# Linear attention and a gated MLP: q loaded in runs of eight tokens on 64 partitions per head, with the remaining token of each run in a chunk of its own

## The chip, the cores and the metric

One core of a Trainium2 chip runs the kernel. The metric is the device time of one execution in microseconds (us); the median of several executions is quoted. An execution counts as slow when it is over 1.5% above the fastest of the same kernel. Comparisons use fast executions alone.

TensorE (PE in the views) does the matmuls and writes their results to PSUM; VectorE (DVE), ScalarE (ACT) and GpSimd (POOL) compute; SyncE (SP) only issues. A DMA is cut into packets, which up to 16 DMA engines carry. It lands when its data are written and those who wait for it may go on. "PE o_ps <- DMA qT_sb" reads: an instruction of PE on tile o_ps waited for a DMA that writes qT_sb.

## The reference, cut to what matters

```python
kv  = einsum('bhsd,bhse->bhde', k, v)          # 8 batches, 8 heads, 576 tokens, 64 wide
o   = einsum('bhsd,bhde->bhse', q, kv)
x   = o / sqrt(mean(o*o, -1) + 1e-6) * g_norm  # per token and head
x   = x.transpose(0, 2, 1, 3).reshape(4608, 512)
h   = x @ w_in                                 # 1024 wide
u   = h * softmax(h)
out = layer_norm(u) * g_ln @ w_out             # 4608 x 512, float32
```

All inputs and the output are float32 in HBM. The 4,608 tokens are 36 tiles of 128.

## The kernel before

The tokens are worked in nine chunks of 512: eight hold the first 512 tokens of one batch each, the ninth holds the last 64 tokens of all eight batches. GpSimd issues the loads, and its DMA converts float32 to bf16. SyncE (SP) issues nearly all stores, and also the five DMA transposes that turn q for chunks 4 to 8. A scheduler in the kernel fixes the order on each engine when the program is built.

```python
XBAR = tuple(range(4, NC))          # chunks whose q is turned by a DMA transpose; NC = 9
bufs = {"k": 3, "v": 3, "q": 3, "qT": 3, ..., "ob": 4}

def load_q(b, hs):                  # token 4p+j of a head on partition p, 128 partitions
    ...
    nc.gpsimd.dma_start(
        T["q", b].rearrange("p h j d -> p h (j d)")[:, hs],
        q[b, :, 0:512, :].rearrange("h (p j) d -> p h (j d)", j=4)[:, hs],
    )

def load_q_last(b):
    nc.gpsimd.dma_start(
        q_last[b:128:B].rearrange("p h j d -> p h (j d)"),
        q[b, :, 512:S, :].rearrange("h (p j) d -> p h (j d)", j=4),
    )

def q_turn(c):
    ...
    nc.sync.dma_start_transpose(
        t.rearrange("q h y p -> q (h y) p"), T["q", c].rearrange("p h j d -> p (h j d)"))

def o_mm(c, hf, tag):               # the last chunk: one matmul of every eighth column per batch
    ...
        for b in [c] if c < B else range(B):
            cols = slice(0, 128) if c < B else slice(b, 128, B)
            ...

def store(c, m):                    # one tile: 128 tokens x 512
    j = 2 * (m % 2) + m // 2
    if c < B:
        dst = out[c * S:c * S + 512, :].rearrange("(p j) d -> j p d", j=4)
    else:
        dst = out.rearrange("(b s) d -> b s d", b=B)[:, 512:S, :].rearrange("b (p j) d -> j p b d", j=4)
    (nc.scalar if c == NC - 1 and m % 2 else nc.sync).dma_start(dst[j], T["ob", c, m][:, :])
```

So before the change the destination of a store is 128 rows, one for each partition of the source tile `ob`, each of 512 floats (2 KB).

The softmax here doesn't subtract the row's maximum and nothing guards it: scores larger than these inputs give would overflow.

## Time and profile before

| | before |
|---|---|
| time, median of 3 | 197.02 us (196.54 to 197.72) |
| span of the profiled execution | 193.1 us |
| TensorE busy | 179.8 us (93%) |
| mean granted clock of TensorE | 0.998 |
| stores | 36 tiles, 9.44 MB |

The next lines are from the page of the kernel before. The first four cut the span into 40 equal slices: TensorE's busy share in tenths, its granted clock in tenths, the mean busy share of the 16 DMA engines in tenths, and GB/s moved. The fifth is the queue that carries the stores and the DMA transposes: packets, MB, and the time that its packets took as a share of 16 engines' span. The last says what the chain that ended last consists of.

```profile
PE   7897997898899998999899999999999999999991
PEclk9999999999999999999999999999999999999999
DMA  1999999999996999899999996363111111211206
GB/s 22 204 204 266 357 203 205 206 224 248 233 201 86 147 190 258 113 185 168 292 214 200 212 111 182 108 116 114 54 54 58 58 54 58 109 58 54 110 7 213
...
q1 hardware_dynamic: 15616, 11.67, 22.4%
...
PE 64%; DMA 20%; ACT 7%; POOL 4%; DVE 2%; issue 2%; SPq 0%; POOLq 0%; DVEq 0%; ACTq 0%
```

TensorE is busy nearly throughout, and from the twenty-ninth slice on the DMA engines have little to do: only stores, which come at the pace of the tiles.

### The profile page before, as it was taken

Reading aid. Unit: us, or ns where it says so; the run is one execution under the profiler, and the core shown is the slowest. Engines: PE = TensorE matmul, PEld = TensorE weight load, DVE = VectorE, ACT = ScalarE, POOL = GpSimd, SP = SyncE. Lnnn points to the kernel's source line nnn. Section 1 sums busy time; section 2 is a strip of 40 time slices with the busy share of each in tenths; the row PEclk is TensorE's granted clock in tenths of the full one; section 3 lists DMA queues with packets and bytes.
Section 4 is the critical chain, followed back from the end, with each engine's and each line's share of the span. In section 5 each row is a group of like instructions: output and inputs, shape, how many; then the busy total and the mean of one; then the engine's idle time right before and its main releaser. Section 6 shows DMA issues by size and latency. Waiting matters only on the chain.

```text
span 193.1 us, 5442 instructions
## 1 busy us (share of the span) xinstructions
PE 179.8 (93%) x2282; PEld 88.3 (46%) x2282; DVE 122.6 (63%) x241; ACT 141.0 (73%) x245; POOL 127.9 (66%) x136
## 2 busy tenths in 40 slices
PE   7897997898899998999899999999999999999991
PEld 2352454553354643544354435445445554544460
DVE  1456588468684887496477658567575747666450
ACT  2038888869895997799689987989789496655520
POOL 7981799500999987977499776568285838846200
PEclk9999999999999999999999999999999999999999
DMA  1999999999996999899999996363111111211206
GB/s 22 204 204 266 357 203 205 206 224 248 233 201 86 147 190 258 113 185 168 292 214 200 212 111 182 108 116 114 54 54 58 58 54 58 109 58 54 110 7 213
DMA packets 36040, 29.71 MB, mean 154 GB/s; under 512 B 11816, under 2 KB 30512, under 8 KB 36016
## 3 DMA queue, kind: packets, MB, share of 16 engines
q0 software_dynamic: 20112, 17.30, 56.4%
q1 hardware_dynamic: 15616, 11.67, 22.4%
q10 hardware_dynamic: 288, 0.39, 0.6%
q8 instruction: 18, 0.29, 0.6%
q14 instruction: 6, 0.05, 0.1%
HBM read 32.51 MB, written 9.44 MB: 217 GB/s over the span
## 4 chain that ended last, share of the span: by engine, by line
PE 64%; DMA 20%; ACT 7%; POOL 4%; DVE 2%; issue 2%; SPq 0%; POOLq 0%; DVEq 0%; ACTq 0%
PE out_ps L582 26%; PE h_ps L468 24%; DMA w_out_f<-in_moe_w_out_dram 9%; DMA v_sb<-in_v_dram 7%; PE misc_ps L534 4%; DMA out_dram<-ob_sb 4%; PE s_ps L369 3%; PE o_ps L348 2%; ACT e_sb L476 2%; PE misc_ps L291 1%; DVE u_sb L483 1%; ACT osq_sb L363 1%; ACT rst_sb L377 1%; ACT lss_sb L373 1%; PE h_ps L592 1%
## 5 line engine op out<-in xcount | busy, mean ns | idle before, releaser
L468 PE MATMUL h_ps<-x_sb,w_in_sb 128*128 128x512 bf16 x276 | 70.3, 379 | 3.0 <-DVE u_sb L483 1.7
L582 PE MATMUL out_ps<-w_out_sb,u_sb 128*128 128x512 bf16 x272 | 69.0, 379 | 0.5 <-issue 0.5
L494 POOL TENSOR_TENSOR usq_sb<-u_sb 128x512 bf16<-128x512 bf16 x50 | 52.0, 1042 | 25.5 <-DVE u_sb L483 25.4
L483 DVE TENSOR_TENSOR u_sb<-h_ps,e_sb 128x512 bf16<-128x512 f32 x69 | 47.3, 688 | 30.4 <-ACT e_sb L476 29.5
L500 POOL TENSOR_TENSOR es_sb<-e_sb 128x512 bf16<-128x512 f32 x36 | 45.9, 1274 | 21.6 <-ACT e_sb L476 21.2
L476 ACT ACTIVATE e_sb<-h_ps,zero_t 128x512 f32<-128x512 f32 x69 | 47.1, 684 | 12.6 <-PE h_ps L468 11.8
L468 PEld LDWEIGHTS <-w_in_sb 128*128 128x128 bf16 x288 | 27.3, 98 | 37.5 <-issue 6.9
L582 PEld LDWEIGHTS <-u_sb 128*128 128x128 bf16 x280 | 26.1, 98 | 31.0 <-issue 2.0
L363 ACT ACTIVATE osq_sb<-o_ps,zero_t 128x512 bf16<-128x512 f32 x31 | 20.1, 683 | 15.3 <-PE o_ps L348 15.3
L614 DVE TENSOR_SCALAR ob_sb<-out_ps,rstd 128x512 f32<-128x512 f32 x33 | 24.6, 745 | 10.0 <-PE out_ps L582 4.3
L390 DVE SCALAR_TENSOR_TENSOR x_sb<-o_ps,g_rep,rst_sb 128x512 bf16<-128x512 f32 x32 | 23.9, 749 | 8.6 <-ACT rst_sb L377 8.4
L377 ACT ACTIVATE rst_sb<-lss_sb,zero_t 128x512 f32<-128x512 f32 x32 | 23.2, 726 | 0.7
L373 ACT ACTIVATE lss_sb<-s_ps,eps_t 128x512 f32<-128x512 f32 x32 | 22.0, 688 | 2.2 <-PE s_ps L369 2.2
L492 ACT ACTIVATE usq_sb<-u_sb,zero_t 128x512 bf16<-128x512 bf16 x22 | 15.8, 719 | 5.4 <-DVE u_sb L483 5.4
L369 PE MATMUL s_ps<-osq_sb,head_mean 128*128 128x512 bf16 x34 | 12.9, 380 | 0.3 <-ACT osq_sb L363 0.3
L534 PEld LDWEIGHTS <-stat_sel 128*32 128x32 bf16 x720 | 10.1, 97 | 3.8 <-issue 3.8
L217 POOL DMA_DIRECT2D k_sb<-in_k_dram x10 | 7.8, 784 | 4.3 <-DMA w_in_sb<-in_moe_w_in_dram 2.9
L198 PE MATMUL s_ps<-zeros 128*128 128x512 bf16 x28 | 9.2, 453 | 1.4 <-DVE zero_t L163 1.2
L225 POOL DMA_DIRECT2D q_sb<-in_q_dram x10 | 8.6, 856 | 2.5 <-DMA w_in_sb<-in_moe_w_in_dram 1.5
L348 PE MATMUL o_ps<-qT_sb,kvd 64*64 64x32 bf16 (+1 forms) x240 | 8.2, 256 | 1.1 <-DMA qT_sb<-q_sb 0.7
L291 PEld LDWEIGHTS <-k_sb 64*64 64x64 bf16 x576 | 6.7, 107 | 4.9 <-issue 4.9
L291 PE MATMUL misc_ps<-v_sb,k_sb 64*64 64x64 bf16 x360 | 7.6, 194 | 0.8 <-DMA v_sb<-in_v_dram 0.7
(85 smaller groups left out, 131.6 us busy)
## 6 DMA issues: line engine op xcount, KB each, us to landing
out_dram<-ob_sb SPq DMA_DIRECT2D x34, 256.0 KB, 2.9
k_sb<-in_k_dram POOLq DMA_DIRECT2D x6, 576.0 KB, 13.3
v_sb<-in_v_dram POOLq DMA_DIRECT2D x6, 576.0 KB, 14.3
q_sb<-in_q_dram POOLq DMA_DIRECT2D x6, 512.0 KB, 15.9
w_out_f<-in_moe_w_out_dram POOLq DMA_DIRECT2D x1, 2048.0 KB, 16.5
k_sb<-in_k_dram POOLq DMA_DIRECT2D x4, 288.0 KB, 11.5
v_sb<-in_v_dram POOLq DMA_DIRECT2D x4, 288.0 KB, 12.2
q_sb<-in_q_dram POOLq DMA_DIRECT2D x4, 256.0 KB, 12.2
```

Of the source, the lines that this page charges most:

```text
L363: nc.scalar.activation(out=t[:, :], in_=T[("o", *i)].rearrange("p a b c -> p (a b c)"), func=AF.Square, bias=zero_t[:, :])
L369: nc.tensor.matmul(t[:, :], head_mean[:, :], T["osq", i][:, :], start=True, stop=True)
L373: nc.scalar.activation(out=t[:, :], in_=T["s", i][:, :], func=AF.Ln, bias=eps_t[:, :])
L377: nc.scalar.activation(out=t.rearrange("p a b c -> p (a b c)"), in_=T["lss", i][:, :], func=AF.Exp, scale=-0.5, bias=zero_t[:, :])
L390: nc.vector.scalar_tensor_tensor(out=T["x", c][:, 2 * hf:2 * hf + 2, z], in0=T["o", c, hf, z][:, :, :, :], scalar=g_rep[:, :], in1=T["rst" ...
L468: nc.tensor.matmul(t[:, :], w_in_sb[:, dt, f * 128:(f + 1) * 128], T["x", c][:, dt].rearrange("p a b c -> p (a b c)"), start=(dt == 0), st ...
L476: nc.scalar.activation(out=T["e", c, f // 2][:, f % 2, :], in_=T["h", c, f][:, :], func=AF.Exp, bias=zero_t[:, :])
L483: nc.vector.tensor_tensor(out=T["u", c][:, f, :], in0=T["h", c, f][:, :], in1=T["e", c, f // 2][:, f % 2, :], op=MUL)
L494: nc.gpsimd.tensor_tensor(out=dst, in0=src, in1=src, op=MUL)
L500: nc.gpsimd.tensor_tensor(out=T["es", c][:, n, :], in0=e[:, 0, :], in1=e[:, 1, :], op=ADD)
L582: nc.tensor.matmul(T["acc", c, m][:, :], T["u", c][:, f, m * 128:(m + 1) * 128], w_out_sb[:, f, :], start=(f == 0), stop=(f == NF - 1),)
L614: nc.vector.tensor_scalar_mul(out=t[:, :], in0=T["acc", c, m][:, :], scalar1=T["rstd", c][:, m:m + 1])
```

## The change

Its intent: q is laid out as k and v already are, two heads side by side on 2 x 64 partitions, and nine consecutive tokens of a head belong to one partition. Eight of them are loaded for the batch's own chunk, in runs of 2 KB rather than 1 KB. The ninth goes to the last chunk, whose columns then keep the batch in the place of the token. That halves the number of matmuls there. The loads for the last chunk move from chunks 2 to 5 to chunks 4 and 5.

```diff
-    def load_q(b, hs):
-        ...
-            q[b, :, 0:512, :].rearrange("h (p j) d -> p h (j d)", j=4)[:, hs],
+    def load(name, src, b, hs):
+        js = 8 if name == "q" else 9
+        ...
+            src[b, hs].rearrange("(n r) (p j) d -> (r p) n (j d)", r=2, j=9)[:, :, 0:js * D],

     def load_q_last(b):
-        nc.gpsimd.dma_start(
-            q_last[b:128:B].rearrange("p h j d -> p h (j d)"),
-            q[b, :, 512:S, :].rearrange("h (p j) d -> p h (j d)", j=4),
-        )
+        nc.gpsimd.dma_start(q_last[:, :, b, :], q[b].rearrange("(n r) (p j) d -> (r p) n j d", r=2, j=9)[:, :, 8, :])
...
-        plan.add(("q_last", b), "pool", 0.6, 2.0 + 0.5 * b, lambda b=b: load_q_last(b),
-                 [("h_mm", 2 + b // 2, 4 * (b % 2))], load=0.5)
+        plan.add(("q_last", b), "pool", 0.7, 4.0 + 0.25 * b, lambda b=b: load_q_last(b),
+                 [("h_mm", 4 + b // 4, 2 * (b % 4))], load=0.7)
... (o_mm: the last chunk has 32 matmuls of 64 columns where it had 64 of 32)
+    def rows_of(c, z, y):
+        if c < B:
+            return out[c * S:c * S + S, :].rearrange("(p j) d -> j p d", j=9)[2 * y + z:2 * y + z + 3:2]
+        return out.rearrange("(b p j) d -> j b p d", p=64, j=9)[8, 2 * y + z:2 * y + z + 3:2]
+
     def store(c, m):
-        j = 2 * (m % 2) + m // 2
-        ...
-        (nc.scalar if c == NC - 1 and m % 2 else nc.sync).dma_start(dst[j], T["ob", c, m][:, :])
+        (nc.scalar if c == NC - 1 and m % 2 else nc.sync).dma_start(
+            rows_of(c, m // 2, 2 * (m % 2)), T["ob", c, m][:, :]
+        )
```

The tile `ob` now holds two tokens' worth of 64 partitions, so the destination of each store is 2 x 64 rows. The bytes and the rows of 2 KB are the same.

More of the change, by code (lines that the diff above doesn't have):

```diff
@@ L147 @@
     kvd = big.tile([128, B, 2, NP, D], BF16, name="kvd")
-    q_last = big.tile([128, H, 4, D], BF16, name="q_last")
+    q_last = big.tile([128, NP, B, D], BF16, name="q_last")
     g_rep = big.tile([128, 1], FP32, name="g_rep")
@@ L210 @@
     plan.add("ident", "pool", 1.0, -1.95, make_ident)
-    def load_kv(name, src, b, hs):
+    def load(name, src, b, hs):
+        js = 8 if name == "q" else 9
         if hs.start == 0:
-            T[name, b] = tile_of((name, b), [128, NP, 9, D], BF16)
+            T[name, b] = tile_of((name, b), [128, NP, js, D], BF16)
         nc.gpsimd.dma_start(
-            T[name, b].rearrange("p n i d -> p n (i d)")[:, hs.start // 2:hs.stop // 2],
-            src[b, hs].rearrange("(n r) (p i) d -> (r p) n (i d)", r=2, i=9),
-        )
-    def load_q(b, hs):
-        if hs.start == 0:
-            T["q", b] = tile_of(("q", b), [128, H, 4, D], BF16)
-        nc.gpsimd.dma_start(
-            T["q", b].rearrange("p h j d -> p h (j d)")[:, hs],
-            q[b, :, 0:512, :].rearrange("h (p j) d -> p h (j d)", j=4)[:, hs],
+            T[name, b].rearrange("p n j d -> p n (j d)")[:, hs.start // 2:hs.stop // 2],
+            src[b, hs].rearrange("(n r) (p j) d -> (r p) n (j d)", r=2, j=9)[:, :, 0:js * D],
         )
     def load_q_last(b):
-        nc.gpsimd.dma_start(
-            q_last[b:128:B].rearrange("p h j d -> p h (j d)"),
-            q[b, :, 512:S, :].rearrange("h (p j) d -> p h (j d)", j=4),
-        )
+        nc.gpsimd.dma_start(q_last[:, :, b, :], q[b].rearrange("(n r) (p j) d -> (r p) n j d", r=2, j=9)[:, :, 8, :])
     def load_w_in(half):
@@ L257 @@
             n = len(heads(b))
-            for i, (name, src) in enumerate((("k", k), ("v", v))):
-                plan.add((name, b, g), "pool", 0.75 if n == 1 else 0.6, at + part + 0.01 * i,
-                         lambda name=name, src=src, b=b, hs=hs: load_kv(name, src, b, hs),
+            for i, (name, src) in enumerate((("k", k), ("v", v), ("q", q))):
+                plan.add((name, b, g), "pool", (0.8 if name == "q" else 0.75) if n == 1 else 0.6, at + part + (0.01 * i if i < 2 else 0.02 if b < 2 else 0.1),
+                         lambda name=name, src=src, b=b, hs=hs: load(name, src, b, hs),
                          behind, uses=[(name, b)] if g else [],
-                         first=[] if g else [(name, b)], load=2.9 / n if b < 3 else 3.5)
-            plan.add(("q", b, g), "pool", 0.9 if n == 1 else 0.7, at + part + (0.02 if b < 2 else 0.1),
-                     lambda b=b, hs=hs: load_q(b, hs), behind,
-                     uses=[("q", b)] if g else [], first=[] if g else [("q", b)], load=2.7 / n if b < 3 else 3.3)
-        plan.add(("q_last", b), "pool", 0.6, 2.0 + 0.5 * b, lambda b=b: load_q_last(b),
-                 [("h_mm", 2 + b // 2, 4 * (b % 2))], load=0.5)
+                         first=[] if g else [(name, b)], load=(2.55 if name == "q" else 2.9) / n if b < 3 else 3.2 if name == "q" else 3.5)
+        plan.add(("q_last", b), "pool", 0.7, 4.0 + 0.25 * b, lambda b=b: load_q_last(b),
+                 [("h_mm", 4 + b // 4, 2 * (b % 4))], load=0.7)
     for half in range(2):
@@ L313, in qT_mm @@
     def qT_mm(c, hf, tag):
-        t = T["qTp", c, hf] = bank((tag,), [128, 4, 2, 128], BF16)
-        for h in range(4):
-            for y in range(2):
-                src = T["q", c][:, 4 * hf + h, 2 * y:2 * y + 2, :].rearrange("p z d -> p (z d)")
-                nc.tensor.transpose(t[:, h, y, :], src, ident[:, :])
+        t = T["qTp", c, hf] = bank((tag,), [128, 2, 4, 128], BF16)
+        for n in range(2):
+            for y in range(4):
+                src = T["q", c][:, 2 * hf + n, 2 * y:2 * y + 2, :].rearrange("p z d -> p (z d)")
+                nc.tensor.transpose(t[:, n, y, :], src, ident[:, :])
     def qT_copy(c, hf):
         if hf == 0:
-            T["qT", c] = tile_of(("qT", c), [128, H, 2, 128], BF16)
-        dst, src = T["qT", c][:, 4 * hf:4 * hf + 4], T["qTp", c, hf][:, :, :, :]
+            T["qT", c] = tile_of(("qT", c), [128, NP, 4, 128], BF16)
+        dst, src = T["qT", c][:, 2 * hf:2 * hf + 2], T["qTp", c, hf][:, :, :, :]
         if c == 1:
@@ L330, in q_turn @@
     def q_turn(c):
-        t = T["qT", c] = tile_of(("qT", c), [128, H, 2, 128], BF16)
+        t = T["qT", c] = tile_of(("qT", c), [128, NP, 4, 128], BF16)
         nc.sync.dma_start_transpose(
-            t.rearrange("q h y p -> q (h y) p"), T["q", c].rearrange("p h j d -> p (h j d)")
+            t.rearrange("q n y p -> q (n y) p"), T["q", c].rearrange("p n j d -> p (n j d)")
         )
     def o_mm(c, hf, tag):
-        ts = [bank((tag,), [128, 2, 2, 128], FP32) for z in range(2)]
+        ts = [bank((tag,), [128, 2, 4, 64], FP32) for z in range(2)]
         for z in range(2):
@@ L342, in o_mm @@
         for pp in range(2):
-            for b in [c] if c < B else range(B):
-                cols = slice(0, 128) if c < B else slice(b, 128, B)
+            n = 2 * hf + pp
+            for y in [slice(0, 4)] if c < B else range(4):
                 for hh in range(2):
@@ L348, in o_mm @@
                         nc.tensor.matmul(
-                            ts[z][hh * 64:hh * 64 + 64, pp, :, cols], kvd[rows, b, hh ^ z, 2 * hf + pp, :],
-                            T["qT", c][rows, 4 * hf + 2 * pp + hh, :, cols], start=True, stop=True,
+                            ts[z][hh * 64:hh * 64 + 64, pp, y, :], kvd[rows, c if c < B else 2 * y + z, hh ^ z, n, :],
+                            T["qT", c][rows, n, y, 64 * hh:64 * hh + 64], start=True, stop=True,
                         )
@@ L375, in s_exp @@
     def s_exp(*i):
-        t = T["rst", i] = tile_of(("rst", i), [128, 2, 2, 128], FP32)
+        t = T["rst", i] = tile_of(("rst", i), [128, 2, 4, 64], FP32)
         nc.scalar.activation(
@@ L381, in s_rsqrt @@
     def s_rsqrt(*i):
-        t = T["rst", i] = tile_of(("rst", i), [128, 2, 2, 128], FP32)
+        t = T["rst", i] = tile_of(("rst", i), [128, 2, 4, 64], FP32)
         nc.scalar.activation(
@@ L388, in x_mul @@
         if (hf, z) == (0, 0):
-            T["x", c] = tile_of(("x", c), [128, NP, 2, 2, 128], BF16)
+            T["x", c] = tile_of(("x", c), [128, NP, 2, 4, 64], BF16)
         nc.vector.scalar_tensor_tensor(
@@ L429 @@
             kvs = [("kv", b, x, part) for b in ([c] if c < B else range(B)) for x in ((hf,) if b < 2 else range(2)) for part in range(3)]
-            plan.add(("o_mm", c, hf), "pe", 0.25 if c < B else 1.2, r + w * (0.35 + 0.5 * hf),
+            plan.add(("o_mm", c, hf), "pe", 0.25 if c < B else 0.6, r + w * (0.35 + 0.5 * hf),
                      lambda c=c, hf=hf, tag=tag: o_mm(c, hf, tag), [("qT", c) if c in XBAR else ("qT", c, hf), *kvs],
@@ L605, in store_cols @@
     def store_cols(x):
-        dst = out.rearrange("(b s) (x d) -> b s x d", b=B, x=2)[:, 512:S, x, :].rearrange("b (p j) d -> j p b d", j=4)[3]
-        (nc.sync, nc.scalar)[x].dma_start(dst, T["ob", NC - 1, 3][:, x])
+        cols = slice(x * d_model // 2, (x + 1) * d_model // 2)
+        (nc.sync, nc.scalar)[x].dma_start(
+            rows_of(NC - 1, 1, 2)[:, :, cols], T["ob", NC - 1, 3][:, x]
+        )
     def scale(c, m):
@@ L614, in scale @@
             nc.vector.tensor_scalar_mul(out=t[:, :], in0=T["acc", c, m][:, :], scalar1=T["rstd", c][:, m:m + 1])
+    def rows_of(c, z, y):
+        if c < B:
+            return out[c * S:c * S + S, :].rearrange("(p j) d -> j p d", j=9)[2 * y + z:2 * y + z + 3:2]
+        return out.rearrange("(b p j) d -> j b p d", p=64, j=9)[8, 2 * y + z:2 * y + z + 3:2]
     def store(c, m):
-        j = 2 * (m % 2) + m // 2
-        if c < B:
-            dst = out[c * S:c * S + 512, :].rearrange("(p j) d -> j p d", j=4)
-        else:
-            dst = out.rearrange("(b s) d -> b s d", b=B)[:, 512:S, :].rearrange("b (p j) d -> j p b d", j=4)
-        (nc.scalar if c == NC - 1 and m % 2 else nc.sync).dma_start(dst[j], T["ob", c, m][:, :])
+        (nc.scalar if c == NC - 1 and m % 2 else nc.sync).dma_start(
+            rows_of(c, m // 2, 2 * (m % 2)), T["ob", c, m][:, :]
+        )
     plan.add("w_mean", "pe", 2.0, -0.5, lambda: [w_mean(f) for f in range(NF)], ["w_out", "g_mean", ("o_mm", 0, 1)],
```

## The prediction

> **What bounds the kernel now.** I read three things in this order: the busy time by stretch of the run, the chain that ended last, and then the DMA queues, because the change touches every load of q and every store. The busy times of three stretches (length; busy us and instruction count of each engine; granted TensorE clock; DMA share; GB/s):
>
> ```profile
> 0.00:38.00 38.00, 33.01 (x388) 16.52 (x388) 20.93 (x50) 22.67 (x38) 28.61 (x40) 1.00 1.13 208
> 38.00:97.00 59.00, 54.91 (x737) 26.59 (x737) 41.71 (x77) 49.96 (x90) 41.06 (x41) 1.00 1.17 196
> 97.00:193.00 96.00, 91.87 (x1159) 45.24 (x1158) 59.92 (x115) 68.39 (x119) 58.18 (x55) 1.00 0.44 106
> ```
>
> Up to 38 us the DMA is full (share 1.13) and PE waits for loads; part of its 33 us is filler on a tile of zeros. From 97 us on PE is busy 92 of 96 us and the DMA only 0.44: PE is the bound and stores are hidden. In the chain, in order of time (start, us, what), the pieces that the change touches:
>
> ```profile
> 25.06 13.71 DMA v_sb<-in_v_dram
> ...
> 87.76 7.72 DMA out_dram<-ob_sb
> ...
> 144.52 1.06 PE o_ps L348 x64
> ...
> 154.36 1.07 PE o_ps L348 x57
> ```
>
> So the start hangs on a v load that queues behind two batches of q; one place hangs on a store that was issued late behind a DMA transpose; and the last chunk spends two times 1.06 us on 64 small matmuls. Otherwise the chain is h and out matmuls back to back.
>
> Now the stores. Of the output tensor's instructions, the issue row, then the row of waits and the landing times, and then a stretch of 4 us in which one store of 256 KB runs alone:
>
> ```profile
> L623 SPq DMA_DIRECT2D out_dram<-ob_sb x34: 332/332/1017, 38.7 to 187.7; - x34
> ...
>   DVE ob_sb L614: 2.0, 1
> ...
> DMA to landing us min/median/max: 2.0/2.9/8.0
> ```
>
> ```profile
> DMA  0000000000008989995100000000000000000000
> ...
> q1 hardware_dynamic: 144, 0.26, 16.9%
> ```
>
> The first store goes out at 38.7 us, one lands 2.9 us after its issue, and in the whole run DVE waited once, 2.0 us, for a store to free its buffer. In the second view the store is 144 packets: 128 rows of 2 KB and 16 more, which I read as one completion from each of 16 DMA engines. Their time is 16.9% of 16 engines over 4 us, 10.8 engine-us, so 84 ns for a row of 2 KB, and with 8 rows per engine the store is over in 0.7 us. The same count is in the stretch from 5 to 10 us, which holds the load of g_rows, 8 rows of 512 B, on that queue:
>
> ```profile
> q1 hardware_dynamic: 16, 0.00, 0.5%
> ```
>
> 16 packets are 8 rows and 8 completions, not 16: that DMA ran on 8 engines.
>
> **What the Trainium skill says.** "DMA: Bandwidth & Descriptors", section "Why a DMA increments its semaphore by 16 and not by 1": the number of engines, k, is the largest up to 16 that divides the size of the slowest dimension (not of size 1) of both access patterns, as the instruction carries it; and on the queues of SP and ACT it is always the lowest-numbered k engines. The trace agrees where it can: k = 16 for stores of 128 rows, k = 8 for 8 rows. No run here shows k = 2 yet. The section "Rules for kernel authors" of that page draws the consequence: an outermost dimension of c < 16 confines the whole DMA to at most c engines. "Queues, rings and completion order": an engine takes turns between the queues it has work for. The trace agrees: from 43 to 45 us, when a store and loads run together, the packets of both queues alternate. "Specifications" puts line rate at descriptors of 512 B and more; this bears on q_last, and no run shows it yet.
>
> **The change part by part.**
>
> 1. Loads of q: 512 descriptors of 2 KB read and 1 KB written in place of 1,024 half as long. In the DMA-bound start the queue moves 204 GB/s of bf16 on k, v and w_in and about 195 when q is passing, so a batch of 0.52 MB should fall from 2.69 to 2.57 us, 0.12 us. Two batches lie before the v load in the chain: gain 0.25 us.
>
> 2. The last chunk's o matmuls: 64 of 32 columns become 32 of 64 columns, twice. The kv matmuls, of the same 64x64x64 form, run 72 in 0.70 us (38.91 to 39.61 us), 9.7 ns each: 32 are 0.31 us. The ordinary o group of the same total columns takes 0.34 us. Gain (1.06 - 0.34) x 2 = 1.4 us, on PE and on the path.
>
> 3. q_last: 8 loads of 512 runs of 128 B in place of 128 runs of 512 B, now in chunks 4 and 5, after all k, v, q loads. They leave the stretch from 64 to 88 us, in which the transposes and loads crowd. At most the 2.0 us DVE wait and the 1.0 us of PE idleness near 95 us go. Their small runs cost more DMA time: I estimate 3 us per engine in all.
>
> 4. The stores. This is the part that the title does not name. Tokens of a head lie in runs of nine per partition now, with 64 partitions per head, so one output tile is two slabs of 64 rows. The built program of the changed kernel shows the destination of every store as 2x64x512, where before it was 128x512 (and 16x8x512 in the last chunk). The slowest dimension is 2; the tile's is 128; the largest common divisor up to 16 is 2. By the skill's rule each store runs on two engines, and on the same two each time. The rows stay 2 KB, so a store has 64 rows per engine: 64 x 84 ns = 5.4 us in place of 0.7.
>
> What part 4 costs. A chunk has 4 stores, 21.5 us of these two engines, and PE needs about 17 us per chunk: the stores alone are slower than PE. The tile of the output has 4 buffers, so DVE, then PSUM, then PE stop behind them. The end is set by what these two engines have to do from the first store on:
>
> - first store at 38.7 us;
> - 36 tiles' worth of stores x 5.4 us = 194 us;
> - their sixteenth of the loads that are still to come: the trace of before moves 9.35 MB (bf16) on the load queue from 38.4 us on, at 204 GB/s 46 us;
> - five DMA transposes: the one near 128 us runs alone for about 2.6 us, five are 13 us; they stand in the same SP queue;
> - q_last's extra 3 us, and 2 us from the last packet to the landing.
>
> Sum 38.7 + 194 + 46 + 13 + 3 + 2 = 297 us. I count these as serial on an engine because from 43 to 45 us, where stores and loads are mixed, the DMA moves 284 GB/s by destination, about 390 by what is read (the loads read fp32 and write bf16), no more than the 408 of loads alone. Since every load waits for its slowest engine, k, v and q come later too, but that fills the gaps rather than adding to the sum. The gains of 1 to 3 lie beside the stores and vanish. Of the sum I take off a little, since some loads go by before the first store's packets start; I say 294 us.
>
> **The rivals.**
>
> - Rival A, the stores spread over 16 engines after all (the two slabs are split further somewhere). For it: the last chunk's 16x8x512 stores run well in the trace before, so three dimensions as such do no harm. Against it: 16 divides by 16, so they are no counterexample, and g_rows on 8 engines is the rule at work. Then only 1 to 3 count: 197.0 - 0.25 - 1.4 - up to 1 = about 195 us.
> - Rival B, two engines per store, but not always the same two. Then a store is 5.4 us long, but four may be in flight, 4 per 17 us are needed, and PE stays the bound; only the last store costs about 5 us more: about 200 us. Against it: the skill says the lowest-numbered ones.
> - Rival C, two engines, but with idle gaps between: SP issues in order, and a transpose that waits for its q load holds back finished stores behind it. SP waited 30 us on q loads before. Were half of that to leave the two engines empty, the time would be 310 us.
> - Rival D, that the schedule alone matters: the order on PE, ACT and SP moves from chunk 3 on. PE's work is the same and its idle time after 39 us is about 3 us in all, so this is worth up to 2 us either way.
>
> **Range and chances.** I give the two-engine reading with fixed engines about 87%. Within it, 84 ns may be 78 or 90 ns (14 us either way), and gaps and overlaps are worth some 15 us. So 262 to 325 us should hold eight times in ten. The remaining 13% are mostly rivals A and B: within 2%, with a small part faster.
>
> **What would show it.** Right: a store lands some 8 to 20 us after its issue in place of 2.9; its packets are 130 and not 144; the DMA moves about 50 GB/s at a share of about 0.13 in long stretches late in the run; DVE waits for the output's DMAs for tens of us; the chain is mostly the store; PE's busy share falls to some 60%. Each step by itself: the o groups of the last chunk near 0.34 us; the v load in the chain landing 0.2 to 0.3 us earlier. Wrong: stores of 144 packets that land in 3 us (rival A), or long stores without DVE waits (rival B). Were the DMA idle on its two engines for long while SP waits on q, rival C holds.

## The result

| | before | after |
|---|---|---|
| time, median (range) | 197.37 us (196.54 to 201.81), 4 runs, the longest slow | 293.38 us (293.06 to 294.12), 4 runs |
| span of the profiled execution | 193.1 us | 291.7 us |
| mean granted clock of TensorE | 0.998 | 0.849 |
| output | correct | correct |

The ratio is 1.489, with a 95% interval of 1.483 to 1.496. Ratios here and below are the mean time of one kernel's fast runs over that of the other's fast runs of the same rounds, so they are not quite the ratios of the medians quoted.

The same lines of the page, of the kernel after:

```profile
PE   8889898999500099995416968984599699640000
PEclk9999999999955589999575989999599899795555
DMA  6999999959119993291977982191311111111111
GB/s 96 198 320 230 207 208 218 165 96 200 36 36 54 151 180 92 53 159 36 146 89 67 50 113 58 49 68 51 89 53 51 51 53 51 53 52 51 51 51 38
...
q1 hardware_dynamic: 15126, 11.67, 35.4%
...
DMA 72%; PE 12%; POOL 3%; DVE 3%; ACT 2%; issue 1%; SPq 1%; DVEq 0%; POOLq 0%
```

The chain went from TensorE to the DMA. The ten slices before the last, 73 us, run at 51 to 53 GB/s without a break, at a DMA share of one tenth. TensorE's clock is granted at about half in the slices where it stands idle. The clock can be little of the loss: TensorE's busy time grew by 12.5 us (179.8 to 192.3), its idle time by 86.

The busy times by stretch (length; busy us and instructions of PE, PEld, DVE, ACT, POOL; granted clock; DMA share; GB/s). The first three stretches are those that the prediction shows of before:

```profile
0.00:38.00 38.00, 32.93 (x386) 16.83 (x387) 20.46 (x49) 22.24 (x36) 28.09 (x40) 1.00 1.13 210
38.00:97.00 59.00, 36.44 (x489) 17.87 (x488) 30.31 (x54) 34.24 (x62) 29.56 (x29) 0.86 1.14 122
97.00:193.00 96.00, 71.22 (x842) 32.33 (x842) 41.35 (x83) 53.41 (x95) 44.22 (x44) 0.85 0.87 95
```

Up to 38 us nothing is different: 32.93 us of TensorE against 33.01. The loss begins with the first store. From 38 to 97 us TensorE does 36 us of work where it did 55.

Pieces of the chain that ended last, in order of time (start, us, what):

```profile
42.60 27.73 DMA out_dram<-ob_sb
70.33 31.10 DMA qT_sb<-q_sb
...
115.52 24.14 DMA out_dram<-ob_sb
...
251.16 18.65 DMA out_dram<-ob_sb
```

The stores in this chain take 12 to 28 us from issue to landing, and one DMA transpose 31 us. The stores of the output, from the view of its tensor: the issue row (min/median/max ns of an issue, first and last start in us), then the wait row.

```profile
L613 SPq DMA_DIRECT2D out_dram<-ob_sb x34: 511/4177/11207, 39.1 to 261.3; - x34
...
  DVE ob_sb L603: 65.7, 19
```

The issue itself is now held up for 4.2 us as a rule, against 0.33 before, and VectorE waited 65.7 us, in 19 places, for a store to give its buffer back, against 2.0 us once. Last, 4 us late in the run (219 to 223 us) in which only stores move:

```profile
DMA packets 100, 0.20 MB, mean 51 GB/s; under 512 B 0, under 2 KB 0, under 8 KB 100
...
q1 hardware_dynamic: 100, 0.20, 13.1%
```

That is 100 rows of 2 KB in 4 us, and a share of 13.1%, which is 2.1 of 16 engines. On two engines a row comes every 80 ns.

There is one thing that the prediction did not have. The view of the DMA from 70 to 90 us, in 40 slices of 0.5 us:

```profile
GB/s 204 212 198 207 131 48 38 30 38 36 36 36 36 35 34 38 30 38 36 36 38 30 42 37 33 33 37 37 37 37 35 37 35 37 38 31 33 50 63 58
...
q1 hardware_dynamic: 921, 0.60, 114.9%
q0 software_dynamic: 524, 0.54, 16.1%
```

From 73 to 88 us only some 36 GB/s move, less than the 51 of stores alone: in the packet records some 170 rows of stores (0.35 MB) and as many packets of loads (0.19 MB). They come two at a time, rows and load packets in turn, 180 ns for one of each. So two engines work without a gap, on stores and on their share of the loads, and of the loads issued from 77 us on nothing else moves before 88. Still the packets of the queue of stores and transposes take 114.9% of 16 engines over these 20 us. In the packet records of the trace, 19 packets of the DMA transpose start near 72 us and end together near 88.4 us, 15.5 to 16.4 us each, where the median of such a packet is 18 ns. In the kernel before the longest takes 2.0 us. So a DMA transpose stands still beside these stores, and loads with it. What this is worth is the question of the last experiments.

### The profile page after: what moved, and what is told of

It reads as the page before. It is cut to its first block, busy times and chain, and to the rows that moved or that the text cites. A ratio compares the mean times of both kernels' runs of the same rounds, so it can differ in the third digit from the quotient of the medians.

```text
span 291.7 us, 5315 instructions
## 1 busy us (share of the span) xinstructions
PE 192.3 (66%) x2218; PEld 92.0 (32%) x2218; DVE 122.2 (42%) x241; ACT 141.7 (49%) x245; POOL 128.8 (44%) x136
## 3 DMA queue, kind: packets, MB, share of 16 engines
HBM read 32.51 MB, written 9.44 MB: 144 GB/s over the span
## 4 chain that ended last, share of the span: by engine, by line
DMA 72%; PE 12%; POOL 3%; DVE 3%; ACT 2%; issue 1%; SPq 1%; DVEq 0%; POOLq 0%
DMA out_dram<-ob_sb 49%; DMA qT_sb<-q_sb 11%; DMA v_sb<-in_v_dram 7%; DMA qT_sb<-q_last 5%; PE out_ps L569 4%; PE h_ps L455 4%; DVE ob_sb L603 1%; PE o_ps L335 1%; PE misc_ps L521 1%; POOL k_sb L218 1%; DVE x_sb L377 1%; PE misc_ps L198 1%; SPq L320 1%; POOL usq_sb L481 1%; PE s_ps L356 1%
## 5 line engine op out<-in xcount | busy, mean ns | idle before, releaser
L455 PE MATMUL h_ps<-x_sb,w_in_sb 128*128 128x512 bf16 x276 | 74.4, 395 | 16.0 <-DVE u_sb L470 12.3
L569 PE MATMUL out_ps<-w_out_sb,u_sb 128*128 128x512 bf16 x272 | 74.5, 400 | 2.9 <-DVE u_sb L470 2.9
L455 PEld LDWEIGHTS <-w_in_sb 128*128 128x128 bf16 x288 | 28.0, 100 | 54.1 <-issue 26.3
L569 PEld LDWEIGHTS <-u_sb 128*128 128x128 bf16 x280 | 27.1, 102 | 38.4 <-issue 8.7
L335 PE MATMUL o_ps<-qT_sb,kvd 64*64 64x256 bf16 (+1 forms) x176 | 8.3, 269 | 38.7 <-DMA qT_sb<-q_sb 24.1
L335 PEld LDWEIGHTS <-kvd 64*64 64x64 bf16 x192 | 4.0, 115 | 45.9 <-issue 38.2
L521 PEld LDWEIGHTS <-stat_sel 128*32 128x32 bf16 x720 | 11.4, 104 | 4.0 <-issue 4.0
L278 PE MATMUL misc_ps<-v_sb,k_sb 64*64 64x64 bf16 x360 | 8.2, 194 | 3.3 <-issue 2.3
## 6 DMA issues: line engine op xcount, KB each, us to landing
k_sb<-in_k_dram POOLq DMA_DIRECT2D x6, 576.0 KB, 16.1
```

Of the source, the lines that this page charges most:

```text
L455: nc.tensor.matmul(t[:, :], w_in_sb[:, dt, f * 128:(f + 1) * 128], T["x", c][:, dt].rearrange("p a b c -> p (a b c)"), start=(dt == 0), st ...
L569: nc.tensor.matmul(T["acc", c, m][:, :], T["u", c][:, f, m * 128:(m + 1) * 128], w_out_sb[:, f, :], start=(f == 0), stop=(f == NF - 1),)
```

## The experiments

Twelve runs were made, in four batches on three chips; each batch has its own runs of the kernel before. The table says which kernel each starts from. One more idea, to put the rows into pairs in VectorE's multiplication, did not build, since the operands had too many dimensions.

| run | what it is | median us of all runs (number) | ratio to before, fast runs |
|---|---|---|---|
| e1 | after, each store as two of 64 rows | 193.48 (4) | 0.993 (0.984 to 1.002) |
| e1 again | the same, five rounds | 193.67 (6, one slow) | 0.9895 (0.9861 to 0.9928) |
| e2 | after, rows in pairs, 64x2x512 | 194.26 (4) | 0.996 (0.987 to 1.004) |
| e3 | before, batch stores 2x64x512 | 275.8 (2) | 1.413 (1.397 to 1.430) |
| e4 | before, batch stores 4x32x512 | 213.62 (4) | 1.095 (1.087 to 1.104) |
| e11 | before, batch stores 8x16x512 | 204.54 (5, three slow) | 1.034 (1.011 to 1.056) |
| e5 | after, batch stores from GpSimd | 236.36 (the fast one of 2) | none |
| e10 | e5, last chunk's stores split as in e1 | 216.82 and 219.18 (the fast two of 4) | 1.114, no interval |
| e8 | e4 with its stores on ScalarE's queue | 215.38 (the fast one of 4) | none |
| e9 | e1 with q_last loaded early again | 195.17 (6) | 0.9985 (0.9953 to 1.0017) |
| e12 | before, no DMA transposes | 198.99 (4) | 1.018 (1.011 to 1.025) |
| e13 | e12 with batch stores 4x32x512 | 206.84 (4) | 1.059 (1.053 to 1.065) |

**Theory and rival.** The theory is the prediction's: the slowest dimension of the destination, 2, confines each store to two engines, and this alone is the loss. The rival is that something else in the new layout costs the time: the small q_last loads, the order of the schedule, or stores of more than two dimensions as such.

### e1: the same rows, two stores of 64 rows each

```diff
-        (...).dma_start(rows_of(c, m // 2, 2 * (m % 2)), T["ob", c, m][:, :])
+        for i in range(2):
+            (...).dma_start(rows_of(c, m // 2, 2 * (m % 2))[i], T["ob", c, m][64 * i:64 * i + 64, :])
```

(and the same for the last tile, which is stored in two halves of its columns)

> The changed kernel with each store issued as two DMAs of 64 rows, one per slab, so that the slowest dimension is 64 and not 2; the bytes, the order of the engines and everything else stay. My theory (a store on two engines is the whole loss): 16 completions per store again, a store lands in about 3 us, DVE no longer waits for stores, and the time falls from 293 us to 195 us (193 to 198), a little under the kernel before, because the gains of the o matmuls (1.4 us) and of q (0.25 us) are then on the path. Rival (the loss is in the new layout itself: the q loads, the small runs of q_last or the moved schedule): stays above 250 us.

It took 193.48 us and is correct. The whole loss of 96 us is gone, although everything else of the change is still there. The issue row and the landing times of the output's DMAs:

```profile
L615 SPq DMA_DIRECT2D out_dram<-ob_sb x68: 466/584/1316, 39.0 to 185.6; - x68
...
DMA to landing us min/median/max: 2.2/2.8/6.9
```

(this is from the repeat of e1). Twice as many stores land in 2.8 us each, and no engine waits for one. In the chain of e1 the o matmuls of the last chunk are these two pieces, with their new duration:

```profile
145.24 0.38 PE o_ps L335 x32
...
152.67 0.38 PE o_ps L335 x32
```

Together they were 1.06 + 1.07 = 2.13 us and are 0.76, a gain of 1.37 us.

### e3: the kernel before, with nothing but the shape of the store changed

```diff
-            dst = out[c * S:c * S + 512, :].rearrange("(p j) d -> j p d", j=4)
+            dst = out[c * S:c * S + 512, :].rearrange("(p x j) d -> j x p d", x=2, j=4)
```

This puts rows at the wrong tokens. The last chunk's four stores are left alone.

> The kernel before with one edit: the destination of the 32 stores of the first eight chunks is written as 2x64x512 (odd and even groups of rows), so that rows come out in another order; wrong on purpose. q, q_last and the schedule are those of before. My theory: two engines, rows at 80 ns (the cadence that the changed kernel's trace shows), so 32 x 64 x 80 ns = 164 us of stores, with 46 of loads, 13 of transposes and 2 us for the last chunk on the same two engines after the first store at 39 us: 264 us (250 to 280), and DVE waits for stores. Rival (the layout of q is needed for the loss): about 197 us.

It took 275.8 us. So the shape does it without the rest of the change, and the rival falls. The size fits too: the change confines four more stores, and 4 x 64 rows x 80 ns is 20.5 us, which would make 296 us. Less the 2 us that the rest of the change turned out to be worth (below), that is 294, and the changed kernel takes 293.4.

### e2: pairs of rows together, with 64 outermost

The o matmuls write their PSUM columns in such an order that a tile's partitions 2p and 2p+1 hold neighbouring tokens of the output. A store is then one DMA of 64x2x512.

```diff
-                            ts[z][hh * 64:hh * 64 + 64, pp, y, :], ...
+                            to if c < B else to[:, y // 2, y % 2, :], ...      # to: columns at a step of two
...
-            rows_of(c, m // 2, 2 * (m % 2)), T["ob", c, m][:, :]
+            rows_of(c, m // 2, 2 * (m % 2)).rearrange("y p d -> p y d"), T["ob", c, m][:, :]
```

> The changed kernel with the two tokens of an output tile interleaved: PE writes its columns pairwise, so that a store is still one DMA but of 64x2x512 in place of 2x64x512, same rows and same places in memory. My theory: 64 and 128 have 16 as common divisor, so 16 engines, 194 to 198 us as in e1. Rival (three-dimensional destinations, or rows 18 KB apart, are what is slow): about 290 us, as the number of dimensions and the row addresses are the same as in the changed kernel.

It took 194.26 us and is correct: three dimensions as such do no harm when 64 is the outer one. It has a small price that was not foreseen. The o matmuls of 256 columns, first in e2, then in e1 (shape, count, busy us, mean ns of one):

```profile
L337 PE MATMUL o_ps<-qT_sb,kvd 64*64 64x256 bf16 x112 | 9.2, 408 | 0.6 <-ACT qT_sb L313 0.5 <-DVE x_sb L379 0.2
```

```profile
L335 PE MATMUL o_ps<-qT_sb,kvd 64*64 64x256 bf16 x112 | 6.1, 281 | 0.7 <-ACT qT_sb L313 0.5 <-DVE x_sb L377 0.3
```

The same matmul takes 408 ns in place of 281 when it writes every other column of PSUM.

### e4 and e11: four and eight engines

The same edit as e3 with x=4 and x=8, also wrong.

> As e3 but 4x32x512, wrong on purpose. The rule of the slowest dimension says four engines: 4 completions per store, a lone store lands in 32 x 80 ns + 2 us = 4.6 us. The four engines then have 82 us of stores, 46 of loads and 13 of transposes after 39 us, 141 us, less than the 154 us that PE needs: the time is near that of before, 197 to 207 us, with the loss in the stretch where loads run. Rival (any destination whose slowest dimension is under 16 costs alike): 260 us and more. Rival (the number of engines doesn't matter as long as stores are asynchronous): 197 us.

> Wrong on purpose (rows land at other tokens). The kernel before with its 32 batch stores as 8x16x512. Theory A (the slowest dimension sets the number of engines): 8 engines, 80 packets+completions by the trace 136 per store, 16 rows per engine, 1.3 us per store in place of 0.65. Their low engines carry 32 x 16 x 80 ns = 41 us over the run, half of what four engines had, so 196 to 202 us. Rival (any three-dimensional destination of rows suffers, in proportion to its steps): more than 213 us, as with 4x32x512.

The cost falls with the number of engines: ratios of 1.41, 1.095 and 1.034 for two, four and eight. The packet records show the number itself: while stores run, the count of rows in flight that is seen for the longest is two in e3 (147 us), four in e4 (63 us) and eight in e11 (26 us, in a slow run). The rival of e11, that any such destination suffers in proportion to its steps, falls. But e4, with 213.62 us, lies well above its expectation of 197 to 207, and the fast runs of e11 (201.26 and 203.37) lie at the upper end of its 196 to 202 and above it. On four engines the stores are 32 tiles x 32 rows x 80 ns = 82 us of work for each of them, far less than the span, so the sum that explains two engines does not explain this. What TensorE waited for in e4 (us in all, times, longest):

```profile
PE o_ps L348 <- DMA qT_sb<-q_sb: 13.3, 3, 5.0
```

It waited 0.7 us for transposes in the kernel before. So the excess shows as waits for DMA transposes, those that were seen to stand still above. In the packet records, the time of the transposes' packets, summed over all engines, is 282 us in the kernel before, 661 in e4, 1,002 in e3 and 1,260 in the kernel after.

### e8: are the transposes late because they queue behind stores on SP?

```diff
-        (nc.scalar if c == NC - 1 and m % 2 else nc.sync).dma_start(dst[j], T["ob", c, m][:, :])
+        (nc.scalar if c < B or m % 2 else nc.sync).dma_start(dst[j], T["ob", c, m][:, :])
```

This is e4 with the stores issued from ScalarE, so that SP issues only the transposes.

> e4 (4x32x512, wrong on purpose) took 213.6 us where I expected 197 to 207; PE waited 13.3 us there for DMA transposes. Theory A: on the four engines the transposes stand in SP's ring behind the stores. With the 32 stores issued by ACT, in a ring of their own, the engines take turns, the transposes come sooner: 198 to 205 us, though ACT has 32 x 0.54 us of issue more. Theory B: it is the loads that come late on the four busy engines, and the transposes only pass that on: the time stays at 211 to 216 us.

Its one fast run took 215.38 us, where theory B had it; the other three were slow. TensorE waited 22.8 us for transposes in the profiled run, a slow one. The order on SP is thus not shown to be the cause. But ScalarE spent 0.55 us on the issue of each of 33 stores, 18 us in all, so the run is not a clean refutation, and I count it as inconclusive. In the packet records of that slow run the longest packet of a transpose takes 2.9 us, against 9.8 in e4, but all of them together take 689 us against 661.

### e12 and e13: no DMA transposes at all

```diff
-    XBAR = tuple(range(4, NC))
+    XBAR = ()
```

TensorE then turns q in every chunk. e12 is the control, e13 has the stores of e4 besides.

> The kernel before with no DMA transposes: chunks 4 to 8 have q turned by TensorE as chunks 0 to 3 do. Correct. TensorE gets 80 more transposes, some 5 us, VectorE 10 more copies of 0.69 us. 199 to 204 us. It is the control for the next run.

> The same without DMA transposes, and the 32 batch stores as 4x32x512 (wrong on purpose). With DMA transposes this shape of store cost 17.4 us. Theory A (a DMA transpose stands still on all 16 engines while four of them have store rows to do, and TensorE waits for it): without transposes the cost is gone, this run within 4 us of its control. Theory B (late loads of k, v, q on the four engines, or the stores themselves, are the cost): 10 us or more above the control.

They took 198.99 and 206.84 us, 7.9 us apart, 4.0% by the ratios (1.059 over 1.018). The same stores cost 9.5% where the transposes were DMAs. The result lies between the two theories: more than half of the cost of four-engine stores goes away with the DMA transposes, and the rest does not. Where the rest is, the waits of TensorE and the chain of e13 tell:

```profile
PE misc_ps L319 <- DMA q_sb<-in_q_dram: 5.9, 2, 5.7
```

```profile
36.75 32.42 DMA q_sb<-in_q_dram
```

A load of q is 32 us on its way and TensorE stands idle 5.7 us for it. In the control the only such wait is 0.4 us, before a weight load. So late loads are the second part: they too have rows on the four engines that the stores keep busy. How much of the fall is due to e12's extra work on TensorE, which can hide some waiting, no run separates.

What a transpose that stands still waits for, the packet records tell in part. In the kernel after, e3 and e4, twelve times packets of a transpose stay in flight for over 2.4 us. Each time they end together 0.2 to 0.5 us after the last row of a store, and the next row starts at least 1.4 us later. So a standstill lasts until the rows of the stores issued before have run out. Why the transpose's packets on the other engines wait with it stays open.

### e5 and e10: the same 2x64x512 stores, from GpSimd

The Trainium skill, "DMA: Bandwidth & Descriptors", section "Why a DMA increments its semaphore by 16 and not by 1", says that on GpSimd's queue a DMA of k < 16 engines runs on k neighbouring engines from a cursor that goes round. Then two engines per store should hurt less.

```diff
-        (nc.scalar if c == NC - 1 and m % 2 else nc.sync).dma_start(
+        (nc.gpsimd if c < B else nc.scalar if m % 2 else nc.sync).dma_start(
             rows_of(c, m // 2, 2 * (m % 2)), T["ob", c, m][:, :]
```

> The changed kernel with the 32 stores of the first eight chunks issued by GpSimd in place of SP, destinations 2x64x512 as they are. The skill says that a DMA of GpSimd on k engines takes them from a cursor that moves round. My theory (what costs is that every store goes to the same two engines): a store still lasts 5 us and more, but the stores spread: 196 to 215 us, with 32 x 0.8 us of issue more on GpSimd, which has a third of its time free. Rival (a store of two slabs is slow whoever issues it, or the cursor doesn't move): 270 us and more.

e5 took 236.36 us in its fast run: better than 293, but far above the expectation. Here are its two stretches, up to the last store from GpSimd and after it:

```profile
0.00:204.00 204.00, 178.08 (x2107) 85.21 (x2108) 119.97 (x233) 138.97 (x241) 154.09 (x167) 0.96 1.04 138
204.00:234.60 30.60, 6.51 (x112) 3.98 (x110) 2.74 (x8) 2.14 (x5) 0.88 (x2) 0.68 0.18 57
```

By 204 us all but 6.5 us of TensorE's work is done. Then come the last chunk's four tiles, left on SP and ACT, and so on the same two engines: 4 x 5.1 = 20 us, which the expectation forgot. e10 splits these stores as e1 does:

```diff
+        for i in range(2):
+            (nc.scalar if m % 2 else nc.sync).dma_start(dst[i], src[64 * i:64 * i + 64, :])
```

> The last experiment with GpSimd's stores took 236 to 241 us, of which some 20 us at the end were the last chunk's four stores on two engines. Here GpSimd still issues the 32 stores of the first eight chunks as 2x64x512, and the last chunk's are split into DMAs of 64 rows. Theory A (two engines per DMA is the cost, and GpSimd's queue moves on to another pair each time): the tail goes, 212 to 220 us. Rival (GpSimd's stores are slow for another reason, for instance all on the same two engines but started earlier): no less than 232 us.

Its fast runs took 216.82 and 219.18 us, within theory A's range, and the tail is gone. The time after 204 us is 13 us in the profiled run, where it was 30.6. So 32 stores that each run on two engines cost some 80 us from SP's queue (e3) and about 22 us from GpSimd's (24 against e1, which differs in the batch stores alone). The packet records show the spread: in e5 GpSimd's stores are packets of 4 KB at 159 ns each, the same 80 ns for 2 KB, and two of them are in flight for 40 us, four for 36 us, six or eight for 10 us. With SP's queue in the kernel after it is two for 163 us, three for 14 us and hardly ever more, though several stores wait. This agrees with the skill's cursor: what hurts is less the number of engines per store than that they are the same two each time. Of the 22 us that are left, TensorE's waits for DMA transposes are 14.3 us; GpSimd, which also computes, waited 18.3 us for tiles to store. These overlap, and I have not separated them.

### e9 and e1 again: what the rest of the change is worth

```diff
-        plan.add(("q_last", b), "pool", 0.7, 4.0 + 0.25 * b, lambda b=b: load_q_last(b),
-                 [("h_mm", 4 + b // 4, 2 * (b % 4))], load=0.7)
+        plan.add(("q_last", b), "pool", 0.7, 2.0 + 0.5 * b, lambda b=b: load_q_last(b),
+                 [("h_mm", 2 + b // 2, 4 * (b % 2))], load=0.7)
```

> e1 with one part of the change undone: the loads of q_last are put back at the places that they have in the kernel before (from the third chunk on, between the loads of k, v and q). If loading late matters: 0.5 to 2 us slower than e1. If it is hidden anyway: within 0.5 us of e1.

> e1 once more, for a narrow interval and beside e9. With the stores on 16 engines the rest of the change should gain what I predicted, 1.65 us to 2.65 us: a ratio of 0.987 to 0.992 to the kernel before.

e1 took 193.67 us, 1.05% less than the kernel before, and the interval excludes equality. It is faster than the kernel before by 2 us. With the loads put back early (e9) it takes 195.17 us, which is not to be told from the kernel before. So loading q_last late is worth 1.6 us by the medians of the fast runs, 1.8 by the ratios. A piece of e9's chain that e1's does not have:

```profile
60.37 16.06 DMA qT_sb<-q_sb
```

The longest transpose takes 16.1 us there and 14.4 in e1. The first packets of q_last start at 73.3 us in e9, near this one's end, so those loads may delay it by the 1.7 us; that this is the whole effect is not shown. Besides, e9 has the new, small runs early; the old runs of 512 B early are the kernel before, so the two effects of that load, its size and its time, are not separated.

## Why the prediction was right

The prediction was 294 us; the kernel takes 293.38.

- **Two engines per store: right, and it decides.** e3 shows that the shape suffices for the loss, and e1 that without it there is none. The late stretch has the share of two engines (13.1%). The two stores on ACT's queue have 260 packets where they had 288: 2 x (128 rows + 2 completions) in place of 2 x (128 + 16). That they are always the same two rests on the skill, on the sum below, and on the rows in flight, two on SP's queue even while several stores wait, more on GpSimd's (e5). So rivals A and B fell; rival D falls with e1, which has the new schedule and not the loss.
- **The term "36 tiles' worth of stores": a little too large.** A row comes every 80 ns and not every 84, so a store is 5.1 us in place of 5.4. All stores, 9.44 MB at 51 GB/s, are 185 us in place of 194.
- **The other terms: nearly right in sum, not one by one.** From the first store's issue at 39.1 us to the end of the span are 252.6 us. Less 185, there remain 67.6 us for loads, transposes, q_last and the end, where the prediction had 46 + 13 + 3 + 2 = 64. The packet records split them in part. In five stretches, 24.5 us in all, no row of a store is on its way; each begins when a DMA transpose ends its standstill. So the transposes, with the loads beside them, take 24.5 us and not 13, and 43 us are left for the other loads, q_last and the end, where the prediction had 51. Of these only q_last can be read alone: 4,096 packets of 128 B at a median of 32 ns, 135 us over all engines or 8.4 us on each, where 1,024 packets of 512 B at 60 ns were 3.8 us. That is 4.6 us more, in place of 3. The corrected sum, 39 + 185 + 64 + 1.6, is 290 us against a span of 291.7, and a timed run is some 2 us longer than its span. So the near hit of the total owes something to errors of opposite sign.
- **"That fills the gaps rather than adding to the sum": right for the total, but the picture was too simple.** While a DMA transpose stands still, up to 16.4 us, its packets are in flight, and loads move on two engines at most. As the end is set by the two engines' work, this adds little here. With four engines, where the sum does not set the end, it is more than half of the cost (e4 against e13).
- **Rival C did not come.** From 73 to 88 us the two engines move 36 GB/s, not 51, but they have no gap: rows take turns with load packets, as the sum had it. Late in the run there is no gap either. SP did hold back stores, as the median issue of 4.2 us shows, but they were not missed.
- **The gains of parts 1 to 3 vanish beside the stores: right.** Their worth is seen in e1, 1.05% or 2.0 us, where the prediction's parts add up to 2.65. Part 2 gave 1.37 us of its 1.4. Part 3 gave 1.6 to 1.8 us by e9, where rival A's sum had up to 1. Part 1 is not shown. Its sign did not come: the v load in the chain lands at 39.04 us in the changed kernel (25.15 + 13.89), not 0.2 to 0.3 us before the 38.77 of the kernel before. And the kv matmuls of batch 2 start at 38.91 us before, at 39.17 us in the changed kernel and at 38.41 us in e1, single traces which differ by more than the 0.25 us in question. The three are measured in different ways and overlap in q_last, so they need not add up.
- **Signs foretold.** TensorE's share fell to 66%, not some 60%; the chain is the DMA for 72%; stores take 12 to 28 us in the chain from issue to landing, where 8 to 20 was said. The time in which an issue was held up is in this, and the prediction had left it out.

## What to carry to other kernels

When a layout changes, look at the destination of every store as it is built, before counting any gain: an outermost dimension of two turned a gain of 1% into a loss of 49%, and issuing each slab as a DMA of its own (64 rows, a multiple of 16) brought the gain back. Count the work of the busiest DMA engine and not of all sixteen; if that sum passes the compute, it sets the time. Where it does not, look at what shares those engines, above all DMA transposes and loads that an engine waits for.

## What the Trainium skill lacked or had wrong

- "DMA: Bandwidth & Descriptors", "DMA Transpose (X-bar)": it lacks that a DMA transpose beside stores confined to few engines can stand still. Here its packets stayed in flight for up to 16.4 us (2.0 us before), until the rows of the stores issued ahead of it had run out, and the transposes' packet time grew from 282 to 1,260 us summed over engines. More than half of the 9.5% that four-engine stores cost goes away when TensorE does the transposes (4.0% are left).
- The same page, "Rules for kernel authors": the rule on the outermost dimension held in every run, but it gives no size. Here stores of 256 KB on 8, 4 and 2 fixed engines made the kernel 1.034, 1.095 and 1.413 times as long, and split in two DMAs of 64 rows they land in 2.8 us (median) without a wait.
- The same page, "Why a DMA increments its semaphore by 16 and not by 1": nothing found wrong. It does not say how much the cursor of GpSimd's queue softens the case: 1.114 times before with the batch stores there (e10), against 1.413 on SP's queue (e3).
- "PSUM — Partial Sum Buffer", "Specifications (TRN2)", says that any access pattern that is not contiguous slows matmuls significantly, but not by how much: with columns at a step of two, a matmul of 256 columns took 408 ns in place of 281 (e2).
